# Block-sparse attention with experts: the blocks' own keys first, v by halves of heads, another first batch, and constant products in TensorE's planned waits

## The chip, the cores and the metric

One core of one Trainium2 chip. The metric is the device time of one launch in microseconds (us). TensorE (PE) multiplies matrices and transposes, VectorE (DVE), ScalarE (ACT) and GpSimd (POOL) work on rows, SyncE (SP) issues DMAs; POOL issues DMAs too, on a queue of its own. Each engine works through its own instructions in the order in which the program was written; semaphores hold it where it needs another engine's result or a DMA's.

## The reference

Four batches, eight heads, 768 tokens, 64 channels per head. A token attends to the tokens less than 16 away and to one summary of each of the 24 blocks of 32 tokens (the maximum of k in the block, the mean of v). Each batch then goes to one of eight experts, chosen from its mean.

```python
k_sum = k.reshape(B, H, nb, block, D).max(axis=3)      # block 32, nb 24
v_sum = v.reshape(B, H, nb, block, D).mean(axis=3)
mask_l = np.abs(pos[:, None] - pos[None, :]) < window  # window 16
scores_s = scale * np.einsum('bhsd,bhnd->bhsn', q, k_sum) + np.log(block)
a = softmax(concat([where(mask_l, scale * q @ k^T, -1e9), scores_s]))
x = a @ concat([v, v_sum])                   # then heads side by side: (B, 768, 512)
logits = x.mean(axis=1) @ w_gate             # e = argmax, p = softmax(logits)[e]
out = p * (relu(x @ w1[e]) @ w2[e])          # w1 512x1024, w2 1024x512
```

## The kernel before

Tokens are taken in 12 tiles of 64 queries (j). A tile's keys are a window of 96: its own 64 and 16 on either side. With the 24 block summaries behind them they make 120 rows, so that one product gives all scores of a tile, and one product with v (`av`) the sums and, in a 65th column of ones, the denominators.

A batch passes through these steps, for four pairs of heads:

- **T**: `tk` (line 407) transposes k on TensorE, 16 products into the one PSUM buffer `kps`; `ek` (424 or 426) copies it as overlapping windows to `kT`; `tq` (432) and `eq` (440) do the same for q; `km` (446, DVE) takes each block's maximum of k, `kb` (456, ACT) copies it into each window.
- **Q**, for each half of the tiles (first or second): `qk` (464), 12 products into the one buffer `sc`; `ex` (475, ACT) the exponential; `mk` (479, DVE) the mask.
- **A**, for each half: `av` (497), 12 products into the one buffer `ops`; `nm` (510, 511, DVE) divides by the denominators.
- **X**: `tx` (521) transposes the result back and `xc` (529, ACT) copies it to `xT_b`, with sums for the mean.

For v, `load_v` (213, 216, 225) fetches each head into `v_f`, `cast_v` (299, DVE) makes bf16 of two heads at a time in `vblk`, `halo_v` (304, 305, on SP's queue) copies the 16 border rows of each tile from its neighbours, `vs` (359) sums the blocks on TensorE with the 0/1 matrix `bind`, `ev` (369, DVE) copies the sums out, and `bc` (375, on SP's queue) writes them behind each window. In the first batch 80 rows of each tile come from memory, the 16 before it among them.

The gate of a batch: `lgf` (634) four small products, `mxf` (644 to 649, DVE) the copy and the maximum, `ldf` (654, POOL) reads the index, and POOL issues the chosen expert's loads: w1 (665, in two halves for the first batch) and w2 (671). The experts' step then has 16 groups of hidden products (726, here **h**, four products of 512 or of 256 columns each into one of three buffers `hps`), ReLU on ACT (741), 48 output products (760, **o**, eight to a group), the scaling (770) and the store (773).

`Sched` (lines 22 to 132) sets the order. Each step is an operation with an engine, an estimated time and its predecessors; the planner simulates the engines and writes, at each point, the operation that is ready with the longest remaining tail, so that the expert products of one batch lie among the attention steps of the next. PSUM buffers are booked in the planner (`sch.slot`) and taken from rotating pools in the program. POOL issues the loads of the first batch, then k, q and all of v of the second; two small copies (317, 319) hold the issues of the first batch's k and q until v's heads 2 and 6 have landed. Behind each gate's weights follow the loads of the batch after the next.

## Time and profile before

Three runs took 201.25, 202.06 (the median) and 208.47 us. The profiled execution took 201.35 us by the same clock; from its first to its last instruction its span is 199.8 us.

| | VectorE's copy of the gate's logits | first hidden product after it |
|---|---|---|
| first batch | 44.01 us | 59.18 us |
| second | 77.71 | 95.02 |
| third | 122.07 | 135.42 |
| fourth | 160.22 | 172.93 |

Of the span TensorE is busy 160.0 us (80%), VectorE 100.7, ScalarE 95.7, GpSimd 42.4. The chain of waits that ends last has 55% TensorE and 25% DMA. Times are counted from the span's start. In a list of instructions a row has the start, the duration, the engine, the line, the operation with its output and inputs, a count where several are drawn together, and in brackets how long the engine had been idle and what ended that. In the chain a row has start, duration and what held things up there. A releaser is inferred from semaphores; matmul ends are modelled.

### The profile page before, as it was taken

Reading aid. Unit: us, or ns where it says so; the run is one execution under the profiler, and the core shown is the slowest. Engines: PE = TensorE matmul, PEld = TensorE weight load, DVE = VectorE, ACT = ScalarE, POOL = GpSimd, SP = SyncE. Lnnn points to the kernel's source line nnn. Section 1 sums busy time; section 2 is a strip of 40 time slices with the busy share of each in tenths; the row PEclk is TensorE's granted clock in tenths of the full one; section 3 lists DMA queues with packets and bytes.
Section 4 is the critical chain, followed back from the end, with each engine's and each line's share of the span. In section 5 each row is a group of like instructions: output and inputs, shape, how many; then the busy total and the mean of one; then the engine's idle time right before and its main releaser. Section 6 shows DMA issues by size and latency. Waiting matters only on the chain.

```text
span 199.8 us, 4547 instructions
## 1 busy us (share of the span) xinstructions
PE 160.0 (80%) x1902; PEld 93.0 (47%) x1924; DVE 100.7 (50%) x209; ACT 95.7 (48%) x182; POOL 42.4 (21%) x67
## 2 busy tenths in 40 slices
PE   0342877765989799999999899958999995399992
PEld 0231666544365475434556454334556542156440
DVE  5472488599386789311898781563797210000000
ACT  2203267442057676513778736223888642056431
POOL 6126934007420520911025001100000030000000
PEclk9999999999999999999999999996999999579999
DMA  5999999915999999899999957799200039980142
GB/s 86 210 179 156 178 227 214 166 32 80 178 179 225 198 175 151 138 191 257 267 239 191 184 78 208 147 218 242 39 3 0 3 111 229 260 137 0 56 153 111
DMA packets 28689, 30.45 MB, mean 152 GB/s; under 512 B 9756, under 2 KB 22812, under 8 KB 28572
## 3 DMA queue, kind: packets, MB, share of 16 engines
q0 software_dynamic: 14800, 19.40, 59.6%
q1 hardware_dynamic: 13868, 10.75, 21.3%
q8 instruction: 15, 0.25, 0.5%
q14 instruction: 6, 0.05, 0.1%
HBM read 36.06 MB, written 6.29 MB: 212 GB/s over the span
## 4 chain that ended last, share of the span: by engine, by line
PE 55%; DMA 25%; DVE 6%; SPq 4%; issue 3%; ACT 3%; POOL 2%; POOLq 1%; ACTq 0%
PE hps L726 23%; PE hps L760 15%; DMA w_sb<-in_moe_w_dram 11%; DMA v_f<-in_v_dram 7%; DMA q_nat<-in_q_dram 4%; PE ops L359 4%; PE sc L464 4%; SPq L216 3%; PE ops L497 3%; DMA vblk<-vblk 2%; PE kps L407 2%; PE tps L521 2%; PE tps L432 2%; DVE kT L426 1%; DVE xs L511 1%
## 5 line engine op out<-in xcount | busy, mean ns | idle before, releaser
L726 PE MATMUL hps<-xT_b,w_sb 128*128 128x256 bf16 (+1 forms) x239 | 50.3, 343 | 9.3 <-DMA w_sb<-in_moe_w_dram 7.9
L760 PE MATMUL hps<-w_sb,hT_sb 128*128 128x512 bf16 x187 | 43.4, 380 | 0.3
L741 ACT ACTIVATE hT_sb<-hps 128x512 bf16<-128x512 f32 x64 | 29.8, 490 | 23.4 <-PE hps L726 22.5
L726 PEld LDWEIGHTS <-w_sb 128*128 128x128 bf16 x256 | 23.3, 102 | 24.1 <-DMA w_sb<-in_moe_w_dram 7.9
L475 ACT ACTIVATE aT<-sc 128x768 bf16<-128x768 f32 x32 | 25.9, 809 | 15.7 <-PE sc L464 15.6
L770 ACT ACTIVATE o_sb<-hps,gcol 128x512 f32<-128x512 f32 x24 | 16.5, 687 | 28.2 <-PE hps L760 16.4
L760 PEld LDWEIGHTS <-hT_sb 128*128 128x128 bf16 x192 | 18.0, 98 | 20.5 <-issue 0.9
L213 POOL DMA_DIRECT2D v_f<-in_v_dram x24 | 18.0, 761 | 36.4 <-DMA w_sb<-in_moe_w_dram 26.0
L359 PE MATMUL ops<-vblk,bind 80*32 80x512 bf16 (+1 forms) x60 | 16.3, 445 | 6.0 <-DVE vblk L299 6.0
L479 DVE TENSOR_TENSOR aT<-aT,mask 120x768 bf16<-120x768 bf16 x32 | 17.6, 552 | 4.6 <-ACT aT L475 4.4
L426 DVE COPY kT<-kps 128x1152 bf16<-128x1152 bf16 x12 | 16.2, 1349 | 6.3 <-PE kps L407 6.3
L665 POOL DMA_DIRECT2D w_sb<-in_moe_w_dram x5 | 3.8, 753 | 72.3 <-PE hps L760 51.4
L299 DVE CAST vblk<-v_f 80x1536 bf16<-80x1536 f32 x16 | 14.9, 951 | 7.7 <-DMA v_f<-in_v_dram 7.7
L511 DVE TENSOR_TENSOR xs<-ops,rv 128x384 bf16<-128x384 f32 x32 | 17.8, 558 | 1.1
L407 PE MATMUL kps<-identb,k_nat 96*64 96x96 bf16 x256 | 11.3, 249 | 8.5 <-DMA k_nat<-in_k_dram 7.2
L497 PE MATMUL ops<-vblk,aT 120*64 120x65 bf16 x384 | 13.7, 211 | 4.9 <-DVE xs L511 2.0
L529 ACT ACTIVATE xT_b<-tps 128x768 bf16<-128x768 bf16 x16 | 12.9, 809 | 8.9 <-PE tps L521 8.8
L497 PEld LDWEIGHTS <-aT 120*64 120x64 bf16 x384 | 10.0, 122 | 12.9 <-issue 5.0
L464 PE MATMUL sc<-qT,kT 64*128 64x64 bf16 x384 | 13.1, 210 | 2.9 <-ACT kT L456 1.2
L446 DVE TENSOR_REDUCE kmx<-kT 128x24 bf16<-128x768 bf16 x16 | 15.2, 948 | 0.1
L407 PEld LDWEIGHTS <-k_nat 96*64 96x64 bf16 x256 | 9.2, 139 | 10.6 <-DMA k_nat<-in_k_dram 7.2
L464 PEld LDWEIGHTS <-kT 64*128 64x128 bf16 x384 | 9.2, 105 | 10.0 <-issue 6.4
(55 smaller groups left out, 113.8 us busy)
## 6 DMA issues: line engine op xcount, KB each, us to landing
w_sb<-in_moe_w_dram POOLq DMA_DIRECT2D x7, 1024.0 KB, 15.8
out_dram<-o_sb SPq DMA_DIRECT2D x24, 256.0 KB, 5.1
v_f<-in_v_dram POOLq DMA_DIRECT2D x24, 192.0 KB, 11.2
k_nat<-in_k_dram POOLq DMA_DIRECT2D x6, 384.0 KB, 10.3
q_nat<-in_q_dram POOLq DMA_DIRECT2D x6, 384.0 KB, 11.3
v_f<-in_v_dram SPq DMA_DIRECT2D x7, 240.0 KB, 7.2
vblk<-vblk SPq DMA_DIRECT2D x6, 178.8 KB, 6.2
w_sb<-in_moe_w_dram POOLq DMA_DIRECT2D x2, 512.0 KB, 9.4
```

The costliest lines, as they stand in the source:

```text
L213: nc.gpsimd.dma_start(v_f[16:80, :, h, :], v[b, h].rearrange("(j p) d -> p j d", p=QB))
L359: nc.tensor.matmul(ps[0:32, 0 : n * D], lhsT=bind[:, j, :], rhs=vblks[b % 2][0:80, j, hs, 0:D], start=(j == 0), stop=(j == NJ - 1),)
L407: nc.tensor.transpose(kps[hh * D : (hh + 1) * D, g, 2 : 2 + SP], qk_nat[b][1][:, 2 * pr + hh, g, :], identb[0:SP, 0:SP],)
L426: nc.vector.tensor_copy(kdst, win)
L464: nc.tensor.matmul(sc[:, hh, jj * QB : (jj + 1) * QB], lhsT=sb["kT"][pr][rs, j, :], rhs=sb["qT"][pr][rs, j, :], start=True, stop=True, til ...
L475: nc.scalar.activation(aT, sb["sc"][:, :, 0 : NH * QB], ACT.Exp, scale=SCALE)
L479: nc.vector.tensor_tensor(out=aT[0:NR], in0=aT[0:NR], in1=mask[:, hf * NH : (hf + 1) * NH, :] .rearrange("p j c -> p (j c)") .unsqueeze(1) ...
L497: nc.tensor.matmul(ops[(j % 2) * QB : (j % 2 + 1) * QB, hh, jj // 2, :], lhsT=aT[0:NR, hh, jj * QB : (jj + 1) * QB], rhs=vb[0:NR, j, 2 * p ...
L511: nc.vector.tensor_tensor(out=sb["xs"][pr][:, hf * NS : (hf + 1) * NS, :, :].rearrange("p s h d -> p h s d"), in0=ops[:, :, :, 0:D], in1=r ...
L726: nc.tensor.matmul(sb["hps"][:, 0 : c1 - c0], lhsT=sb["w1"][:, dt, ft * 128 : (ft + 1) * 128], rhs=sb["xT"][:, dt, c0:c1], start=(dt == 0) ...
L741: nc.scalar.activation(sb["hT"][:, ft, c0:c1], ps["t"][:, 0 : c1 - c0], ACT.Relu)
L760: nc.tensor.matmul(ps["t"], lhsT=sb["hT"][:, ft, st * 128 : (st + 1) * 128], rhs=sb["w2"][:, ft, :], start=(ft == 0), stop=(ft == NFT - 1),)
```

## The change

Seven things are changed together.

- The window now begins with the tile's own 64 keys; the border rows stand at 64 to 95. The block sums (`vs`) read the 64 own rows and need the casts alone, no border copy. `ek` becomes two copies (80 and 16 keys of each tile); the masks are built anew.
- `vblk` and the sums are laid out by halves of heads: a border copy moves contiguous 16-row pieces, two for each half; the broadcast is split in two.
- The first batch loads 64 rows per tile, as the others did. Heads 0 and 1 and w_gate go on SP's queue, the other six heads on POOL's, between the pairs of k and q. The small holding copies are gone.
- The first batch's casts of heads 2, 3 and of 6, 7 go to ACT. Its block sums stay in a tile `vs0` of their own at rows 96 to 119, and each half's `av` gets six further products with it (line 573 of the changed kernel) in place of the broadcast.
- The second halves of the first batch use the pool of `hps` for scores (two tiles, two exponentials) and for `av`. A written order replaces the general one in that batch, and the second batch's casts come after all its normalisations.
- `fill` writes products of a constant 128x128 tile (`idle_in`, line 958) where the planner sees TensorE wait. Each such place takes one tile of the `hps` pool, which the planner doesn't book.
- The planner lets an operation follow another of its own engine with no semaphore time, allows an engine a delay (0.9 or 0.6 us) for a more urgent operation, and gives later attention steps and v a priority of 8.

```diff
...
+    FILL_TO = 45.0
+    DELAY = {"PE": 0.9, "DVE": 0.6, "ACT": 0.6}
...
+        busy = t0["PE"]
 
         def push(op):
             r = max(
-                [d["end"] + self.SEM for d in op["deps"]] + [d["issued"] for d in op["after"]],
+                [
+                    d["issued"] if d["eng"] == op["eng"] and not d["dma"] else d["end"] + self.SEM
+                    for d in op["deps"]
+                ]
...
-                    elif (
-                        start + op["dur"] <= pick[0] + 0.1
-                        or (start < pick[0] and tail[pick[1]["n"]] - tail[op["n"]] < self.URGENT)
+                    elif start < pick[0] and (
+                        start + op["dur"] <= pick[0] + self.DELAY.get(eng, 0.1)
+                        or tail[pick[1]["n"]] - tail[op["n"]] < self.URGENT
                     ):
...
+            if eng == "PE":
+                idle = t - busy
+                busy = t + op["dur"]
+                if t < self.FILL_TO:
+                    self.fill(int((idle - 0.4) / (0.1 if t < 8.0 else 0.08)))
+                else:
+                    self.fill(int((idle - 1.2) / 0.08))
...
-    v_f = const_pool.tile([80, NJ, H, D], FP32, name="v_f")
+    v_f = const_pool.tile([QB, NJ, H, D], FP32, name="v_f")
...
+    idle_in = const_pool.tile([128, 128], BF16, name="idle_in")
+    vs0 = const_pool.tile([128, 2, H // 2, D + 1], BF16, name="vs0")
...
     def load_v(b, h):
-        if b > 0:
-            nc.gpsimd.dma_start(v_f[16:80, :, h, :], v[b, h].rearrange("(j p) d -> p j d", p=QB))
-            return
...
+        eng = nc.sync if b == 0 and h < 2 else nc.gpsimd
+        eng.dma_start(v_f[:, :, h, :], v[b, h].rearrange("(j p) d -> p j d", p=QB))
...
+        keep(bind, [[QB, NJ], [-BLK, 32]], 0, 1)
+        keep(bind, [[-QB, NJ], [BLK, 32]], BLK - 1, -1)
...
     def cast_v(b, c, eng):
-        hs = slice(2 * c, 2 * c + 2)
-        dst = vblks[b % 2][0:80, :, hs, 0:D]
+        hs = slice(2 * (c % 2), 2 * (c % 2) + 2)
+        dst = vblks[b % 2][0:QB, c // 2, :, hs, 0:D]
+        src = v_f[:, :, 2 * c : 2 * c + 2, :]
         if eng is nc.scalar:
-            nc.scalar.activation(dst, v_f[:, :, hs, :], ACT.Copy)
+            nc.scalar.activation(dst, src, ACT.Copy)
         else:
-            eng.tensor_copy(dst, v_f[:, :, hs, :])
...
-    def halo_v(b, hs):
+            eng.tensor_copy(dst, src)
+
+    def halo_v(b, g):
+
         vb = vblks[b % 2]
-        if b > 0:
-            nc.sync.dma_start(vb[0:16, 1:NJ, hs, :], vb[64:80, 0 : NJ - 1, hs, :])
-        nc.sync.dma_start(vb[80:96, 0 : NJ - 1, hs, :], vb[16:32, 1:NJ, hs, :])
-
-    v_loads = []
-    for h in range(H):
-        v_loads.append(add("SP", 0.5, [], lambda h=h: load_v(0, h), dma=1.08, after=v_loads[-1:]))
-
...
+        nc.sync.dma_start(vb[QB : QB + 16, g, 0 : NJ - 1, :, :], vb[0:16, g, 1:NJ, :, :])
+        nc.sync.dma_start(vb[QB + 16 : KW, g, 1:NJ, :, :], vb[QB - 16 : QB, g, 0 : NJ - 1, :, :])
+
+    v_loads = [add("SP", 0.5, [], lambda: load_v(0, 0), dma=1.2)]
+    v_loads.append(add("SP", 0.5, [], lambda: load_v(0, 1), dma=1.2, after=v_loads[-1:]))
+
+    def load_wg():
+        nc.sync.dma_start(wg_sb, moe_w_gate.rearrange("(g p) e -> p g e", p=128))
+
+    wg_load = add("SP", 0.5, [], load_wg, dma=0.2, after=v_loads[-1:])
...
+    def pool_v(h):
+        v_loads.append(add("POOL", 0.75, [], lambda: load_v(0, h), dma=0.95, after=[last]))
+        return v_loads[-1]
...
-    tk = add("POOL", 0.2, [v_loads[2], bind_setup], lambda: nc.gpsimd.tensor_copy(tok[:, 0:1], v_f[:, NJ - 1, 2, 0:1]))
-    qk_loads[0, 1] = add("POOL", 1.3, [tk], lambda: load_qk(0, 2, 4), dma=2.3)
-    tk = add("POOL", 0.2, [v_loads[6]], lambda: nc.gpsimd.tensor_copy(tok[:, 1:2], v_f[:, NJ - 1, 6, 0:1]), after=[qk_loads[0, 1]])
-    qk_loads[0, 2] = add("POOL", 1.3, [tk], lambda: load_qk(0, 4, 6), dma=2.3)
-    qk_loads[0, 3] = add("POOL", 1.3, [tk], lambda: load_qk(0, 6, 8), dma=2.3, after=[qk_loads[0, 2]])
-    order_pool = [qk_loads[0, 3]]
...
+    last = pool_v(2)
+    last = pool_v(3)
+    last = keep_setup = add("POOL", 0.9, [], setup_keep, after=[last])
+    last = qk_loads[0, 1] = pool_qk(1)
+    last = bind_setup = add("POOL", 1.2, [], setup_bind, after=[last])
+    last = qk_loads[0, 2] = pool_qk(2)
+    last = pool_v(4)
+    last = pool_v(5)
+    last = pool_v(6)
+    last = pool_v(7)
+    last = qk_loads[0, 3] = pool_qk(3)
...
-            on_act = False
+            on_act = b == 0 and c % 2 == 1
...
+                    after=norms[0] if b == 1 else [],
...
-            def vs(b=b, hs=hs, n=n, st=st):
+            def vs(b=b, g0=g0, g1=g1, n=n, st=st):
                 ps = ops_pool.tile([128, 512], FP32, name="ops")
+                p0 = KW if b == 0 else 0
...
                     nc.tensor.matmul(
-                        ps[0:32, 0 : n * D],
+                        ps[p0 : p0 + 32, 0 : n * D],
                         lhsT=bind[:, j, :],
-                        rhs=vblks[b % 2][0:80, j, hs, 0:D],
+                        rhs=vblks[b % 2][0:QB, g0:g1, j, :, 0:D].rearrange("p g h c -> p (g h) c")
+                        if g1 - g0 == 1
+                        else vblks[b % 2][0:QB, :, j, :, 0:D],
                         start=(j == 0),
...
-            def ev(b=b, n=n, hs=hs, st=st):
+            def ev(b=b, g0=g0, g1=g1, n=n, st=st):
+                dst, src = (
+                    (vs0[KW:NR], st["ps"][KW:NR]) if b == 0 else (vsbs[b % 2], st["ps"][0:NB])
+                )
...
-            win = bass.AP(
-                tensor=full.tensor,
-                offset=full.offset,
-                ap=[list(full.ap[0]), [QB // G, NJ], [1, KW // G], [SP + 4, G]],
...
+            for a0, n, c0 in ((2, 10, 0), (0, 2, 80)):
+                win = bass.AP(
+                    tensor=full.tensor,
+                    offset=full.offset + a0,
+                    ap=[list(full.ap[0]), [QB // G, NJ], [1, n], [SP + 4, G]],
+                )
+                kdst = kT[:, :, c0 : c0 + n * G].rearrange("p j (a g) -> p j a g", g=G)
...
         def av(pr, hf):
             aT = sb["aT"][pr, hf]
-            ops = sb["ops", pr, hf] = ops_pool.tile([128, 512], FP32, name="ops")[
-                :, 0 : 2 * NS * (D + 1)
-            ].rearrange("p (h s c) -> p h s c", h=2, c=D + 1)
+            if second(pr, hf):
+                ops = mps_pool.tile([128, 512], FP32, name="hps")
+            else:
+                ops = ops_pool.tile([128, 512], FP32, name="ops")
...
+            rows = KW if b == 0 else NR
...
                     nc.tensor.matmul(
                         ops[(j % 2) * QB : (j % 2 + 1) * QB, hh, jj // 2, :],
-                        lhsT=aT[0:NR, hh, jj * QB : (jj + 1) * QB],
-                        rhs=vb[0:NR, j, 2 * pr + hh, :],
-                        start=True,
-                        stop=True,
+                        lhsT=aT[0:rows, hh, jj * QB : (jj + 1) * QB],
+                        rhs=vb[0:rows, h // HW, j, h % HW, :],
+                        start=(b > 0 or (hh == 0 and jj < 2)),
+                        stop=(b > 0),
+                    )
+            if b > 0:
+                return
+            for hh in range(2):
+                h = 2 * pr + hh
+                for s in range(NS):
+                    nc.tensor.matmul(
+                        ops[:, hh, s, :],
+                        lhsT=aT[KW:NR, hh, 2 * s * QB : 2 * (s + 1) * QB],
+                        rhs=vs0[KW:NR, h // HW, h % HW, :],
+                        start=False,
+                        stop=(hh == 1 and s == NS - 1),
+                        tile_position=(KW, 0),
                     )
...
-        sch.prio = 40.0 if b == 0 else 0.0
+        sch.prio = 40.0 if b == 0 else 8.0
...
-        sch.prio = 40.0 if b == 0 else 0.0
...
+            sch.prio = 8.0
             casts, bcs = v_ops(nxt, vl)
+            sch.prio = 0.0
...
+    def fill(n):
+
+        if n < 1:
+            return
+        idle = mps_pool.tile([128, 512], FP32, name="hps")
+        for _ in range(n):
+            nc.tensor.matmul(idle[:, 0:128], lhsT=idle_in, rhs=idle_in, start=True, stop=True)
...
```

**GpSimd, the first batch's loads.** Rows name a line, the operation and its output and input; `tok` are the small holding copies. Before:

```order
L206 DMA q_nat<-in_q_dram 96x2x512
...
L246 AFFINE_SELECT bind<-bind 80x384 x3
L317 CAST tok<-v_f 80x1
L206 DMA k_nat<-in_k_dram 96x2x512
...
L319 CAST tok<-v_f 80x1
L206 DMA k_nat<-in_k_dram 96x2x512
...
L213 DMA v_f<-in_v_dram 64x12x64 x8
```

Now:

```order
L229 DMA v_f<-in_v_dram 64x12x64 x2
L249 AFFINE_SELECT mask_116<-mask_116 96x64 x2
L249 AFFINE_SELECT mask_118<-mask_118 96x64
L222 DMA k_nat<-in_k_dram 96x2x512
L222 DMA q_nat<-in_q_dram 96x2x512
L249 AFFINE_SELECT bind<-bind 64x384 x2
L222 DMA k_nat<-in_k_dram 96x2x512
L222 DMA q_nat<-in_q_dram 96x2x512
L229 DMA v_f<-in_v_dram 64x12x64 x4
L222 DMA k_nat<-in_k_dram 96x2x512
```

No issue waits for a landing any more, and six heads of v stand among those of k and q.

**VectorE, the end of the first batch**, from the last cast for that batch's own v (299 before, 309 now) to the gate's copy. Now:

```order
L309 CAST vblk_103<-v_f 64x12x2x64
L537 TENSOR_TENSOR aT<-aT,mask 120x768 x2
L492 TENSOR_REDUCE kmx<-kT_109 128x24
...
L412 CAST vs_112<-ops 24x4x64
...
L486 COPY qT<-tps 128x768
...
L309 CAST vblk_104<-v_f 64x12x2x64 x3
L760 COPY lg<-ops 1x8
```

Before, the row with three casts in front of `lg` was one cast, a normalisation and two casts (`L299 CAST vblk_104`). From the cast that opens this piece on, there are now eight masks, two key maxima, one query copy, one copy of sums, eight normalisations and four casts.

**TensorE around the gate of the third batch**, one row for each group of equal products (weight loads left out). Before:

```order
L634 MATMUL ops<-wg_sb,pooled 1x8 x4
L760 MATMUL hps<-w_sb,hT_sb 128x512
...
L407 MATMUL kps<-identb,k_nat 64x96
...
L688 MATMUL ops<-grec,ones_row 128x1
...
L359 MATMUL ops<-vblk_104,bind 32x512
...
L464 MATMUL sc<-qT,kT_107 128x64
...
L726 MATMUL hps<-xT_b,w_sb 128x512
```

Now:

```order
L750 MATMUL ops<-wg_sb,pooled 1x8 x4
L478 MATMUL tps<-identb,q_nat 64x12x8
...
L452 MATMUL kps<-identb,k_nat 64x96
...
L872 MATMUL hps<-w_sb,hT_sb 128x512
...
L397 MATMUL ops<-vblk_104,bind 32x512
...
L516 MATMUL sc<-qT,kT_108 128x64
...
L842 MATMUL hps<-xT_b,w_sb 128x512
```

Between gate and next h there were three o groups, two `tk`, two `tq`, one `qk` and the block sums; now there are four o groups, three `tk`, three `tq`, four `qk` and the sums. Counted the same way, the second gate has behind it three o groups, three `tk`, three `tq`, four `qk` and the sums (before: two pairs of h groups, six o groups, `tk`, `tq`, sums), and the first gate two `tk`, three `tq`, two `qk`, the sums and 29 constant products. Ahead of the second gate, from that batch's first h, stand now all eight pairs of h groups, six `qk`, two `tk`, one `tq`, eight `av`, four `tx`, three o groups. Ahead of the first gate there are 124 constant products, 74 of them in front of the first block sums.

## Rows read from the trace of the kernel before

**Rows 1.** The chain of waits, first batch: start, duration, what held there.

```profile
13.01 4.94 DMA vblk<-vblk
...
32.24 8.30 DMA q_nat<-in_q_dram
```

**Rows 2.** GpSimd's instructions of the front; the bracket is idle time and releaser.

```profile
18.66 0.63 POOL L206 DMA_DIRECT2D q_nat<-in_q_dram  x1
19.28 1.29 POOL L206 DMA_DIRECT2D k_nat<-in_k_dram  x1
...
21.22 2.99 POOL L213 DMA_DIRECT2D v_f<-in_v_dram  x4
...
46.15 1.50 POOL L665 DMA_DIRECT2D w_sb<-in_moe_w_dram  x2 [13.23 <-DVE grec L685]
```

**Rows 3.** The page's DMA issues: count, KB each, median us to landing.

```profile
v_f<-in_v_dram POOLq DMA_DIRECT2D x24, 192.0 KB, 11.2
...
v_f<-in_v_dram SPq DMA_DIRECT2D x7, 240.0 KB, 7.2
```

**Rows 4.** VectorE's instructions, first batch.

```profile
19.37 0.96 DVE L299 CAST vblk<-v_f 80x1536 bf16<-80x1536 f32 x1 [3.53 <-DMA v_f<-in_v_dram]
...
25.09 0.95 DVE L446 TENSOR_REDUCE kmx<-kT 128x24 bf16<-128x768 bf16 x1
...
29.16 0.55 DVE L479 TENSOR_TENSOR aT<-aT,mask 120x768 bf16<-120x768 bf16 x1
29.62 0.55 DVE L440 COPY qT<-tps 128x768 bf16<-128x768 bf16 x1
```

**Rows 5.** Windows: us, busy PE, PEld, DVE, ACT, POOL, granted clock, DMA, GB/s.

```profile
23.00:44.00 21.00, 15.49 (x317) 12.57 (x318) 15.87 (x32) 12.41 (x20) 5.55 (x8) 1.00 0.99 170
...
95.00:114.00 19.00, 18.27 (x323) 11.05 (x328) 17.05 (x30) 15.51 (x31) 3.60 (x5) 1.00 1.14 222
```

**Rows 6.** VectorE's instructions at the first three gates.

```profile
44.01 0.15 DVE L644 COPY lg<-ops 1x8 f32<-1x8 f32 x1
...
77.71 0.15 DVE L644 COPY lg<-ops 1x8 f32<-1x8 f32 x1
...
115.69 2.68 DVE L299 CAST vblk<-v_f 80x1536 bf16<-80x1536 f32 x3
...
122.07 0.15 DVE L644 COPY lg<-ops 1x8 f32<-1x8 f32 x1 [3.00 <-PE ops L634]
```

**Rows 7.** DMA issues around the first and second gates' w1 loads.

```profile
w_sb<-in_moe_w_dram POOLq DMA_DIRECT2D x1, 512.0 KB, 8.5
...
w_sb<-in_moe_w_dram POOLq DMA_DIRECT2D x1, 1024.0 KB, 13.1
```

**Rows 8.** The chain of waits, from the first gate's block sums to the end.

```profile
49.67 5.23 PE ops L359 x12
...
85.97 2.73 PE ops L359 x12
...
95.02 0.32 PE hps L726
...
95.98 0.28 PE sc L464 x12
...
96.81 0.46 PE tps L432 x16
...
104.96 0.44 PE tps L521 x6
...
115.82 1.73 PE hps L760 x8
...
124.18 10.97 DMA w_sb<-in_moe_w_dram
...
135.42 0.81 PE hps L726 x3
...
172.93 0.61 PE hps L726
```

More of the change, by code (lines that the diff above doesn't have):

```diff
@@ L323 @@
+    mask_setup = add("DVE", 0.9, [keep_setup], setup_mask)
+    sch.prio = 0.0
+    later_setup = add("DVE", 1.0, [], setup_later)
+    sch.prio = 40.0
+    order_pool = [last]
     v_ready = {}
@@ L458, in qk @@
         def qk(pr, hf):
-            sc = sb["sc"] = sc_pool.tile([128, 2, 512], FP32, name="sc")
+            if second(pr, hf):
+                sc = [mps_pool.tile([128, 512], FP32, name="hps") for _ in range(2)]
+            else:
+                whole = sc_pool.tile([128, 2, 512], FP32, name="sc")
+                sc = [whole[:, 0, :], whole[:, 1, :]]
+                sb["sc"] = whole
+            sb["sc", pr, hf] = sc
             for jj in range(NH):
@@ L536, in attention, with second @@
         act_k = b == 0
+        cold = 1.0
+        def second(pr, hf):
+            return b == 0 and hf == 1
         def add_T(pr):
@@ L559, in add_QK @@
             ts, qts, deps = t
-            ss, sd = sch.slot("sc", 1)
-            o_qk = add("PE", 0.34, deps + sd, lambda: qk(pr, hf), lat=0.2)
+            if second(pr, hf):
+                slots = [sch.slot("mps", 3), sch.slot("mps", 3)]
+            else:
+                slots = [sch.slot("sc", 1)]
+            sd = [d for _, ds_ in slots for d in ds_ if d is not None]
+            o_qk = add("PE", 0.34 * cold, deps + sd, lambda: qk(pr, hf), lat=0.2)
             ts["readers"].append(o_qk)
@@ L564, in add_QK @@
             as_, ad = sch.slot("aT", 5)
-            o_ex = add("ACT", 0.82, [o_qk] + ad, lambda: ex(pr, hf))
-            ss["first"], ss["readers"] = o_qk, [o_ex]
+            o_ex = add("ACT", 0.98 if second(pr, hf) else 0.82, [o_qk] + ad, lambda: ex(pr, hf))
+            for sl, _ in slots:
+                sl["first"], sl["readers"] = o_qk, [o_ex]
             as_["first"] = o_ex
@@ L606, in do, with first_sequence @@
                 add_X(pr, XS[pr])
+        def first_sequence():
+            do("T", 0)
+            do("Q", 0, 0)
+            do("Q", 0, 1)
+            do("T", 1)
+            do("A", 0, 0)
+            do("Q", 1, 0)
+            do("A", 0, 1)
+            do("Q", 1, 1)
+            do("T", 2)
+            do("A", 1, 0)
+            do("Q", 2, 0)
+            do("A", 1, 1)
+            do("Q", 2, 1)
+            do("T", 3)
+            do("X", 0)
+            do("A", 2, 0)
+            do("Q", 3, 0)
+            do("A", 2, 1)
+            do("Q", 3, 1)
+            do("X", 1)
+            do("A", 3, 0)
+            do("A", 3, 1)
+            do("X", 2)
+            do("X", 3)
         def sequence():
+            if b == 0:
+                first_sequence()
+                return
             do("T", 0)
```

189 lines of the change are left out of this document (101 added, 88 removed).

## The prediction

> **What bounds it now.** I read the chain of waits first, since it says what each stage ends on, then the lists of VectorE and GpSimd for the front, the windows for how densely an engine can work, and the DMA issues.
>
> The kernel is one chain of four stages. A gate's copy on VectorE releases the index and the weight loads; their landing and TensorE's leftover work release the next batch's h; h and the attention among it end in the next gate. At the first gate the chain runs through border copies (4.94 us) and the last q load of the second batch (8.30 us) [rows 1], because a cast for the second batch's v stands in front of the gate's copy. VectorE meanwhile stands 3.53 us for v [rows 4]. The second stage is TensorE's own work; the last two end on weights (10.97 us at the third gate [rows 8]). So a gate that comes earlier pays fully where weights bind, and TensorE's order decides what hides them.
>
> **First gate, 44.0 to 37.2.** Without holding copies POOL's issues up to v's head 5 are three pairs of k and q (0.63 us each issue) and four v loads (2.99 us [rows 2]); with some 3 us of selects, from a start at 1.5 us, the last of them is out at about 11 us. A first-batch v load took 7.2 us to land, one on POOL's queue 11.2 [rows 3]; the queue is not yet deep, so I take 7.2, and the third cast starts at 18 (from 16 to 22). Behind it VectorE has, in order, what it had between 23 and 44 us, plus one cast (0.96) and two masks (1.10), less one key maximum (0.95) and two query copies (1.10) [rows 4]: no difference, 15.87 us [rows 5]. In that window it was 76% busy, waiting for TensorE's single buffers; between 95 and 114 us it reached 90% [rows 5]. The second halves' own buffers remove part of these waits. So 17.7 to 21.0 us; I take 19.2, and the copy stands at 37.2 instead of 44.01 [rows 6]. The bounds are 33.7 and 43.
>
> The block sums for `vs0` lie in TensorE's waits there (15.49 us busy of 21 [rows 5]), and so do 48 more `av` products. A constant product has no row; its nearest, a 128x128 transpose, is 0.44/6 = 0.07 us [rows 8]. The 74 ahead of the first sums (5.4 us) lie in the wait for the first loads. The other 50 cost 3.7 us where no wait is left and nothing where one is; I take nothing. The split `ek` (16 more copies on ACT and VectorE) is hidden in the later stages, where VectorE has slack.
>
> **First weights and h, 59.2 to 48.1.** The loads were issued 2.14 us behind the copy [rows 2, 6]: 39.3. Their first half landed 8.5 us on [rows 7]; with the second batch's loads still moving it could be the third gate's 10.97 [rows 8]. I take 8.5, 47.8, and 0.3 to the first product, as between 135.15 and 135.42 [rows 8]. TensorE's work in between is five transposes (0.46), two `qk` (0.28) and the sums (2.73): 5.6 us [rows 8], at 2.4 GHz done long before.
>
> **Second gate, 77.7 to 73.7.** The stage from h to the next gate took 27.05 us in the third [rows 6, 8]. It held the same eight pairs of h, eight `av`, four `tx` and three o, but two more `qk` (0.56) and two more transposes (0.92): 25.6 us. This is longer than the stage was (18.5), for work that stood behind the gate has moved ahead of it: the new stage gains 11.1 us at its start and returns 7.1.
>
> **Second h, 95.0 to 87.8.** Behind the gate remain three o (5.2), six transposes (2.8), four `qk` (1.1) and the sums: 11.8 us, where it was 17.3. Now the weights bind: 2.1 us to the issue and 10.97 to 13.1 to land [rows 7, 8], middle 12.0. What was TensorE's bound becomes a wait of 2 us.
>
> **Third gate, 122.1 to 114.** By TensorE the stage loses four `qk`, three transposes and one o against 27.05, 4.2 us, and ends at 110.6. But the copy stands behind the last cast of the fourth batch's v, the copies of one `kT` and a key maximum. The last cast started at 115.69 + 2/3 of 2.68 = 117.5, 39.8 us behind the second gate's copy [rows 6], and all these loads are issued behind that gate: 113.5, and 3.3 us of VectorE work (0.96, about 1.4, 0.95) give 116.8. Since the queue is emptier at the second gate than it was, I take the middle, 114.
>
> **Third h, 135.4 to 127.3.** 13.35 us behind the copy, as before [rows 6, 8]; TensorE's work behind the gate (four o, six transposes, four `qk`, sums: 13.5 us from 110.6) is done earlier, so weights still decide.
>
> **Fourth h and end.** From third to fourth h it was 37.5 us [rows 8], less three transposes, three `qk` and one o (3.95): 160.9. Then the tail, 199.8 - 172.93 = 26.9: a span of 187.8. The profiled execution lies 1.55 above its span: 189.3. It is 0.7 below the median of 202.06, so **190**.
>
> **Rivals.**
>
> *TensorE stays at 1.2 GHz behind the first gate.* The block sums there took 5.23 us against 2.73 later [rows 8], the lower of its levels, after a front in which TensorE had stood and waited. Then the 5.6 us are 11.2 and the 29 constant products up to 4.3, h starts at about 51 and the result is 193. For it speaks that TensorE was 74% busy in that window already [rows 5]; against it, the constant products fill its pauses.
>
> *The front gives nothing.* The third cast at 22 us and VectorE at 76%: the copy at 43 to 44, h at 54.9, gates at 80.5 and about 121, h at 134.1 and 167.7: 197.
>
> *VectorE blocks POOL's issues.* A k load's issue on POOL took 1.29 us where the one before it took 0.63, while a cast ran on VectorE from 19.37 [rows 2, 4]. If all front issues did so, the ten up to head 5 would cost some 7 us more and this is the second rival again, 197. Four v issues side by side with VectorE's work took 2.99, 0.75 each, so I expect two to four such meetings, 1.3 to 2.6 us, inside the bounds above. The Trainium skill (SBUF — State Buffer, Who interferes with whom) says that VectorE in its two-port mode, casts and copies among them, fully blocks GpSimd, its descriptor writing included, and that a queue not fed by GpSimd avoids it. It speaks against moving six heads from SP's queue to POOL's; the one long issue agrees.
>
> *The shared pool turns against it: slower.* Constant products take tiles of the three `hps` buffers, which now also hold the first batch's second halves; the planner doesn't book them. In order on TensorE, such a tile waits until ACT or VectorE has read the one three back. A round of two exponentials, mask, `av` and normalisation is some 3 us; at seven places that is 21, less the 4 us which they were meant to fill: 17, the first gate at 54 and everything behind it 17 later, **207**. It decides from about 2.3 us at each place. Against it: TensorE has a quarter of that window free [rows 5], and VectorE, not TensorE, is behind.
>
> **Chances.** The forecast with its bounds 0.56; TensorE's clock 0.16; the front gives nothing, blocked issues included, 0.18; the shared pool 0.10, half of it at 2 us or less a place, within 2%. A measurement of this kernel tells 2% from no change: below 198.0 is faster, above 206.1 slower. The first two cases and five ninths of the third are faster: 0.82; same 0.13; slower 0.05. The range: cast at 16 (-3.5) and third gate at TensorE's bound (-3.4) give 183; upwards the second rival with the third gate at 116.8 gives 200.
>
> **What would show it.** Right: the first copy at 35 to 39, the first h within 0.5 us of its weights, the second gate at 73 to 75 with all h groups ahead of it, a TensorE wait of about 2 us for weights at the second gate, the third copy right behind a cast chain. Wrong: idle time in front of line 958 with VectorE or ACT as releaser (shared pool); block sums of 5 us behind the first gate (clock); POOL issues of 1.3 us in a row (blocked issues); VectorE's third cast later than 22.

## The result, and the profile after

The changed kernel took 193.9 us (median of four, 193.2 to 198.3) beside 204.0 for the kernel before on the same chip: a ratio of 0.961, 95% interval 0.953 to 0.969. The forecast was 190, range 183 to 200, faster. The profiled execution is the longest of the four (198.26 us, span 196.0; the others have spans of 191 to 193), so it is compared with before stage by stage, and a second trace of the same kernel (experiment 1) stands beside it.

VectorE's third cast for the first batch's v, and its copies at the four gates; columns as in [rows 6], to which the copies answer:

```profile
20.70 0.94 DVE L309 CAST vblk<-v_f 64x1536 bf16<-64x1536 f32 x1
...
46.54 0.15 DVE L760 COPY lg<-ops 1x8 f32<-1x8 f32 x1
...
83.80 0.14 DVE L760 COPY lg<-ops 1x8 f32<-1x8 f32 x1
...
121.52 0.14 DVE L760 COPY lg<-ops 1x8 f32<-1x8 f32 x1
...
154.68 0.15 DVE L760 COPY lg<-ops 1x8 f32<-1x8 f32 x1 [2.44 <-PE ops L750]
```

From copy to copy the second to fourth batches take 37.3, 37.7 and 33.2 us where they took 33.7, 44.4 and 38.2; the last stage takes 41.3, where it took 39.6. In this trace the first copy does not come earlier at all: 46.5 instead of 44.0. All that this execution wins is won between the second and the fourth gate. Its span is only 3.8 us shorter than before, and the trace of experiment 1 is also of a longest execution; in which stages the rest of the median's gain lies, no trace of the change shows.

The windows of the stages; columns as in [rows 5]:

```profile
15.00:45.00 30.00, 28.00 (x437) 21.99 (x436) 16.96 (x35) 15.00 (x29) 8.75 (x12) 0.50 0.90 142
...
20.70:46.50 25.80, 23.81 (x361) 18.70 (x360) 16.13 (x33) 12.65 (x24) 6.03 (x9) 0.50 0.78 127
...
55.70:80.30 24.60, 24.46 (x338) 13.98 (x340) 16.52 (x33) 16.99 (x35) 5.39 (x7) 1.00 1.15 181
83.80:99.40 15.60, 14.50 (x159) 7.25 (x159) 10.87 (x24) 5.33 (x11) 6.77 (x9) 0.67 1.01 187
99.40:121.20 21.80, 21.18 (x296) 12.46 (x294) 15.44 (x31) 15.96 (x33) 3.63 (x5) 1.00 1.07 196
```

The first row is the front. TensorE is busy 28.0 of 30 us there, at a granted clock of 0.50; VectorE, which the forecast took for the limit, is busy 17.0. The second row is the part from the third cast to the first gate's copy: TensorE 23.8 of 25.8 us, VectorE 16.1. The lower clock level is not new in the front: sixteen transposes of k take 0.85 us in the kernel before (first list) as in the change (second list), though the granted clock reads 1.00 there [rows 5] and 0.50 here.

```profile
23.03 0.85 PE L407 MATMUL kps<-identb,k_nat 96*64 96x96 bf16 x16
```
```profile
28.38 0.85 PE L452 MATMUL kps<-identb,k_nat 96*64 96x96 bf16 x16
```

The two window rows with a clock of 1.00 and next to no idle time are the stages from h to gate, full as forecast.

VectorE's last cast for the third batch's v, in front of the second gate's copy, and TensorE's logits of that gate:

```profile
81.59 0.95 DVE L309 CAST vblk<-v_f 64x1536 bf16<-64x1536 f32 x1 [2.13 <-DMA v_f<-in_v_dram]
82.47 1.41 DVE L472 COPY kT<-kps 128x960 bf16<-128x960 bf16 x2
```
```profile
79.98 0.35 PE L750 MATMUL ops<-wg_sb,pooled 128*1 128x8 f32 x8
```

The logits are there at 80.3; the copy stands 3.5 us behind them, for a load, a cast and a copy of `kT` that the gate does not need.

TensorE's list around the first and the last gate:

```profile
13.65 2.71 PE L397 MATMUL ops<-vblk,bind 64*32 64x256 bf16 x12 [3.41 <-ACT vblk L307]
...
38.65 0.37 PE L958 MATMUL hps<-idle_in 128*128 128x128 bf16 x2 [0.57 <-ACT aT L529]
...
49.96 2.80 PE L397 MATMUL ops<-vblk,bind 64*32 64x512 bf16 x12
...
168.31 7.88 PE L842 MATMUL hps<-xT_b,w_sb 128*128 128x512 bf16 x31 [3.96 <-DMA w_sb<-in_moe_w_dram]
```

The block sums behind the first gate take 2.80 us, where the kernel before needed 5.23 [rows 8]. The constant products wait 0.57 us at most for a tile of the shared pool.

### The profile page after: what moved, and what is told of

Its sections match the earlier page's. It is cut to its first block, busy times and chain, and to the rows that moved or that the text cites. A ratio compares the mean times of both kernels' runs of the same rounds, so it can differ in the third digit from the quotient of the medians.

```text
span 196.0 us, 5020 instructions
## 1 busy us (share of the span) xinstructions
PE 175.2 (89%) x2135; PEld 107.0 (55%) x2135; DVE 102.4 (52%) x223; ACT 99.0 (51%) x192; POOL 46.5 (24%) x70
## 4 chain that ended last, share of the span: by engine, by line
PE 58%; DMA 25%; DVE 7%; issue 3%; POOL 2%; ACT 2%; POOLq 1%; DVEq 0%; ACTq 0%
PE hps L842 18%; PE hps L872 14%; DMA v_f<-in_v_dram 10%; DMA q_nat<-in_q_dram 9%; PE ops L397 7%; DMA w_sb<-in_moe_w_dram 6%; PE ops L561 3%; PE sc L516 3%; PE tps L478 3%; PE kps L452 3%; PE tps L598 3%; DVE vblk L309 2%; PE hps L958 1%; PE hps L561 1%; PE hps L573 1%
## 5 line engine op out<-in xcount | busy, mean ns | idle before, releaser
L842 PE MATMUL hps<-xT_b,w_sb 128*128 128x512 bf16 (+1 forms) x256 | 49.2, 340 | 4.9 <-DMA w_sb<-in_moe_w_dram 4.9
L853 ACT ACTIVATE hT_sb<-hps 128x512 bf16<-128x512 f32 (+1 forms) x64 | 29.6, 491 | 16.0 <-PE hps L842 15.7
L842 PEld LDWEIGHTS <-w_sb 128*128 128x128 bf16 x256 | 23.8, 101 | 20.7 <-DMA w_sb<-in_moe_w_dram 5.2
L882 ACT ACTIVATE o_sb<-hps,gcol 128x512 f32<-128x512 f32 x24 | 16.5, 686 | 32.0 <-PE hps L872 22.1
L229 POOL DMA_DIRECT2D v_f<-in_v_dram x30 | 22.7, 766 | 32.4 <-DMA w_sb<-in_moe_w_dram 14.9
L872 PEld LDWEIGHTS <-hT_sb 128*128 128x128 bf16 x192 | 18.0, 99 | 20.7 <-issue 1.5
L397 PE MATMUL ops<-vblk,bind 64*32 64x512 bf16 (+1 forms) x60 | 16.4, 441 | 3.4 <-ACT vblk L307 3.4
L472 DVE COPY kT<-kps 128x960 bf16<-128x960 bf16 (+1 forms) x24 | 16.9, 744 | 2.4 <-PE kps L452 2.4
L958 PE MATMUL hps<-idle_in 128*128 128x128 bf16 x163 | 16.1, 274 | 2.3 <-DVE warm L241 1.2
L588 DVE TENSOR_TENSOR xs<-ops,rv 128x384 bf16<-128x384 f32 x28 | 15.6, 557 | 1.0
L309 DVE CAST vblk<-v_f 64x1536 bf16<-64x1536 f32 x14 | 13.3, 960 | 4.3 <-DMA v_f<-in_v_dram 4.3
L561 PEld LDWEIGHTS <-aT 120*64 120x64 bf16 (+1 forms) x384 | 9.8, 121 | 10.2 <-issue 4.2
L958 PEld LDWEIGHTS <-idle_in 128*128 128x128 bf16 x163 | 13.5, 126 | 3.1 <-DVE warm L241 1.2
L397 PEld LDWEIGHTS <-bind 64*32 64x32 bf16 x60 | 6.8, 118 | 10.7 <-issue 6.4
L587 DVE RECIPROCAL rv<-ops 128x6 f32<-128x6 f32 x28 | 5.4, 192 | 13.4 <-PE ops L561 11.2
```

The source lines that it names most:

```text
L229: eng.dma_start(v_f[:, :, h, :], v[b, h].rearrange("(j p) d -> p j d", p=QB))
L309: eng.tensor_copy(dst, src)
L397: nc.tensor.matmul(ps[p0 : p0 + 32, 0 : n * D], lhsT=bind[:, j, :], rhs=vblks[b % 2][0:QB, g0:g1, j, :, 0:D].rearrange("p g h c -> p (g h) c")
L472: nc.vector.tensor_copy(kdst, win)
L561: nc.tensor.matmul(ops[(j % 2) * QB : (j % 2 + 1) * QB, hh, jj // 2, :], lhsT=aT[0:rows, hh, jj * QB : (jj + 1) * QB], rhs=vb[0:rows, h // ...
L842: nc.tensor.matmul(ps["t"][:, 0 : c1 - c0], lhsT=sb["w1"][:, dt, ft * 128 : (ft + 1) * 128], rhs=sb["xT"][:, dt, c0:c1], start=(dt == 0), ...
```

## The experiments

Each ran on one chip beside the kernel before; 1 to 4, 5 to 8, 9 to 11 and 12 went together. "Copies" are the times of the four gates' copies in its trace. A ratio is to the kernel before. A trace is one execution: the change's own two have first copies 1.5 us apart, and experiments 3 and 12, whose programs are the same up to the last gate, 2.2 us (42.2 and 44.4). Where two traces differ by 2 or 3 us in the front, that alone shows nothing.

**1. The change again.** No edit.

> The changed kernel once more, unchanged, for a second trace beside the experiments that follow. In the trace at hand its TensorE was busy almost without a gap from 13.65 us to the first gate's copy at 46.5, its products at the lower of the two clock levels (block sums of 256 columns 2.71 us for twelve). If that is how the change always runs, the copy stands at 46 to 47 again and the time is 198; if the shorter runs (193.2 to 194.6) differ in the front's clock, a trace of one of them has the copy at 41 to 43, the second gate's copy at 80 or less and all later stages as long as in the trace at hand. If they differ in the second gate's stage only, the first copy is at 46 to 47 and the second at 80.

193.0 us (191.2 to 196.7), ratio 0.960 (0.947 to 0.974). The trace is again of the longest execution (span 194.9): copies 45.1, 81.8, 119.7, 153.2. It has the same granted clock of 0.50 from 15 to 45 us. The copy lies between the times that were expected, so this trace does not tell where the executions differ.

**2. No constant products.** In `fill`:

```diff
-        if n < 1:
+        if n < 1 or n > 0:
             return
```

> All 163 constant products left out, everything else and the order of the rest unchanged. Theory A: the front is TensorE's own work at the lower clock level, and the 50 constant products behind the first block sums (6 us in the trace) are work on that path, which buys nothing: the first gate's copy comes some 5 us earlier (41 to 42), the stretch from gate to first hidden product is longer by 2 to 4 us without the products that filled it, the result is 1 to 3 us under the change (191 to 193). Theory B: they are what brings the clock up when it comes up: without them the block sums behind the first gate take 5.2 us instead of 2.8 and the first hidden products 0.5 us each, and the time is 2 to 5 us over the change (196 to 199).

194.0 us (191.8 to 194.6 and one outlier of 760.6), ratio 0.961 (0.945 to 0.978): the same time, between the two theories. Copies 42.8, 83.5, 122.8, 155.4, span 192.9. The first copy is 2.3 us earlier than in experiment 1, A's direction, but no more than two traces of one front differ. Behind that gate the work runs at the lower clock level and the second stage takes 40.8 us instead of 36.7 (B):

```profile
46.50 5.30 PE L397 MATMUL ops<-vblk,bind 64*32 64x512 bf16 x12
```

And the last stage is 37.5 us instead of 41.7: its granted clock is 1.00 throughout, although TensorE stood 3.45 us for the last weights.

```profile
167.84 10.57 PE L842 MATMUL hps<-xT_b,w_sb 128*128 128x512 bf16 x64 [3.45 <-DMA w_sb<-in_moe_w_dram]
```

That the ten products behind the last gate cost this is not shown: experiment 5 has no constant products either and stands as long, and its 64 products start at the lower level:

```profile
172.86 11.88 PE L731 MATMUL hps<-xT_b,w_sb 128*128 128x512 bf16 x64 [3.45 <-DMA w_sb<-in_moe_w_dram]
```

So the products gain 4 us in the second stage; where they lose it again, since the time is the same, these traces do not settle.

**3. The gap ahead of the first sums filled.** In `fill`:

```diff
+        fills.append(n)
+        if len(fills) == 2:
+            n += 60
```

> Sixty more constant products (90 instead of 30) in the wait for v ahead of the first block sums, where TensorE stood from 10.24 to 13.65 us in the trace; nothing else changed. Theory A (the clock falls in that pause and the front then stays TensorE-bound at the lower level): with the pause filled the block sums take 1.3 to 1.5 us instead of 2.71, the front runs at the upper level, the first gate's copy comes at 38 to 41 and the time is 3 to 6 us under the change. Theory B (the pause does not decide the clock): block sums stay at 2.7, the copy stays at 46, the time is within 1 us of the change.

192.5 us (191.0 to 193.7), ratio 0.963 (0.952 to 0.974): no measurable gain on the change; the copy lies between the two theories. The trace (span 189.4, copies 42.2, 80.2, 116.6, 150.0) shows the mechanism of A and why it brings little:

```profile
13.43 1.51 PE L397 MATMUL ops<-vblk,bind 64*32 64x256 bf16 x12
...
21.87 1.71 PE L397 MATMUL ops<-vblk,bind 64*32 64x256 bf16 x12
23.51 0.85 PE L452 MATMUL kps<-identb,k_nat 96*64 96x96 bf16 x16
```

With the gap filled, the first sums run at the upper level (1.51 us against 2.71), but around 23 us the products fall to the lower one (sixteen transposes 0.85 us, before and later 0.53) with TensorE busy; the granted clock of 25 to 40 us is 0.50. The copy is 2.8 to 4.3 us earlier than in the two traces of the change; in experiment 12, with the same front, 0.7 to 2.2.

**4. Casts behind the gate.** In `v_ops`, `mx` being the operation with the copy:

```diff
-                    after=norms[0] if b == 1 else [],
+                    after=norms[0] if b == 1 else [state[b - 1]["mx"]] if b > 1 else [],
```

> The casts of the third and fourth batches' v are put behind the preceding gate's copy (an order constraint of the planner; the orders of TensorE and VectorE around those gates change with it). Theory A: the second gate's copy at 83.8 us waits for the last cast and its load (VectorE stood 2.13 us for v, and one kT copy follows), while TensorE had the logits at 80.3; without the cast in front the copy stands 3 to 3.5 us earlier there, TensorE does not stand at the gate and does not drop to the lower clock level behind it, and the time is 4 to 7 us under the change. Rival: the weights of that gate then queue behind the same loads, which end no earlier; the h products of the second batch start when they did (99.4), and the time is within 1 us.

202.8 us, ratio 0.999 (0.986 to 1.011): the whole gain is gone. Copies 43.4, 78.3, 120.9, 160.7. The second stage is 34.9 us, 1.8 to 2.3 shorter where A said 3 to 3.5, and the third and fourth are 42.6 and 39.8, 4.7 and 6.3 longer than in experiment 1, which neither theory foresaw. The planner puts less behind such a gate (at the second, two `tk` and two `qk` instead of three and four), and TensorE stands for the weights there, where in the change it did not:

```profile
91.97 1.89 PE L842 MATMUL hps<-xT_b,w_sb 128*128 128x512 bf16 x4 [2.78 <-DMA w_sb<-in_moe_w_dram]
```

and what was not done there comes later, inside the stages that are full: from the second batch's h to the logits' copy TensorE is busy 27.8 us (91.97 to 120.87), in experiment 1 21.2 (97.88 to 119.72). Some of this is the clock, granted at 0.91 over that stretch and at 1.00 in experiment 1's. A gate 3.5 us earlier is worth nothing if the work that hides its weights does not come with it.

**5. The planner's rules alone**, in the kernel before:

```diff
+    DELAY = {"PE": 0.9, "DVE": 0.6, "ACT": 0.6}
...
-                        start + op["dur"] <= pick[0] + 0.1
+                        start + op["dur"] <= pick[0] + self.DELAY.get(eng, 0.1)
...
-        sch.prio = 40.0 if b == 0 else 0.0
+        sch.prio = 40.0 if b == 0 else 8.0
```

> The kernel before with the planner's rules of the change alone (same-engine predecessors without semaphore time, the delays of 0.9 and 0.6 us, priority 8 for later attention and v); layout of v, loads, first batch and masks as before, no constant products. Its order of TensorE around the second, third and fourth gates is the change's, group for group. Theory P (the time is won in the later batches, by what stands ahead of each gate and behind it): the first copy stays at 43 to 45, the second stage takes 37 to 39 us from copy to copy instead of 44.4, the third 33 to 35 instead of 38.2, and the time is 192 to 196, most of the change's gain. Theory F (the order needs the block sums that wait for no border copy, and the front): block sums or av wait for border copies, the stages stay at 42 and 37, the time is 198 to 202.

199.5 us (196.5 to 201.6), ratio 0.994 (0.984 to 1.003). Copies 44.8, 85.5, 126.6, 160.4, span 198.9. The third and fourth stages (the second and third in the expectation's count) fall to 41.1 and 33.8 us; the second grows by 7 to 40.8, since all h groups now stand ahead of its gate. The fourth is as short as P said, the third is not, and both are paid for in the second: the time is F's.

**6. The planner undone**, all else as in the change: the reverse of the edit above.

> The change with the planner's old rules and priorities; the new layout, loads, first batch and constant products stay. The order of later batches goes back to h groups and o groups behind the second gate. Theory P: the later stages take as long as before (44 and 38 us from copy to copy) and the time is 198 to 202. Theory F: the layout and the front carry the gain, and the time is 193 to 196.

200.3 us (197.4 to 207.0), ratio 0.994 (0.986 to 1.002). Copies 41.3, 73.9, 118.1, 155.4, span 197.6: stages of 32.6, 44.2 and 37.3, as before, and a last one of 42.2. Here the stages and the time are P's, in experiment 5 the time was F's, so neither theory holds for both. Taken at their middle, neither half alone gains 1%, and together they gain 3.9%. Without the rules the planner also writes other numbers of constant products.

**7. Further products left out.** In `av`, the loops over `hh` and `s` run over their last value only: 40 of the 48 products are left out, and with them most of the first batch's block sums.

> In the first batch 40 of the 48 further products with the block sums are left out (part of the computation; its output lacks most of the block summaries there). Theory A (the front is TensorE's own work at the lower clock level): 0.078 us each, some 3 us, come off that path, the first copy stands 2.5 to 3.5 us earlier than in the change's second trace (45.1) and the time falls by 2 to 3 us. Rival (they lie in TensorE's waits for VectorE and ScalarE): the copy moves by less than 1 us and the time not at all.

190.0 us (187.7 to 193.2). Copies 41.5, 78.3, 114.2, 148.2, span 187.7: the first copy 3.6 us before that of experiment 1, the second and third stages 36.9 and 35.9 us. This is A's size, but part of it is the clock: the first sums run at the upper level here (1.50 us against 2.71), the granted value from 15 to 45 us was 0.66 and in experiment 1 0.50, and 1.4 of the 3.6 us are won from the first sums to the second, where only five of the 40 stood. That the products lie on the front's path agrees with the trace; how much they cost is not shown apart from the clock.

**8. v back on SP's queue.** In `load_v`:

```diff
-        eng = nc.sync if b == 0 and h < 2 else nc.gpsimd
+        eng = nc.sync if b == 0 else nc.gpsimd
```

> The first batch's six heads of v back on SP's queue, nothing else moved but what the planner makes of it. Theory A (POOL's issues are not what the front waits for: in the change's trace the third cast follows VectorE's own work without a wait, and the issues on POOL took 0.64 to 0.90 us each): the first block sums start within 1 us of where they did, the first copy moves by less than 1.5 us, the time by less than 1.5. Rival (VectorE blocks POOL's issues and v's loads queue behind k and q there): v's heads 2 and 3 land 2 us earlier or more, the first sums start at 11 instead of 13.2 us and the time falls by 2 us or more.

204.3 us (198.6 to 206.8), against 201.2 for the kernel before on that chip: neither theory. The chain of waits and ScalarE's list:

```profile
7.80 0.95 SPq L229
8.79 22.68 DMA v_f<-in_v_dram
```
```profile
31.56 1.50 ACT L307 ACTIVATE vblk<-v_f 64x1536 bf16<-64x1536 f32 x1 [15.87 <-DMA v_f<-in_v_dram]
```

The last head of v, issued at 8.8 us on SP's queue, lands at 31.5, beside all of k and q and the second batch's loads on POOL's; on POOL's queue, in its place between k and q, the last cast started at 20.5 in experiment 1. The first copy falls back to 55.3. With the holding copies gone, v's place in POOL's queue is worth 10 us of the front.

**9. Sums wait for the border copies again.** The 0/1 matrix gets rows 64 to 95 of zeros, and later batches' sums read them:

```diff
-                        else vblks[b % 2][0:QB, :, j, :, 0:D],
+                        else vblks[b % 2][0:KW, :, j, :, 0:D],
```

> The change, but the block sums of the second to fourth batches read the 32 border rows too (against zeros of the 0/1 matrix, so that the sums are the same) and so wait for the border copies again; the planner knows it. Theory L (what the planner's order wins in the later batches needs sums that wait for no border copy, since the planner alone gave under 1%): the sums behind the gates and the av of the next batch come later, the second and third stages from copy to copy take 39 to 41 us instead of 36.7 and 37.9, the time is 196 to 199. Rival (border copies land in 6 us and the sums stand far enough behind the casts; what the planner lacked alone was TensorE's clock behind the first gate, 5.3 us for the sums there instead of 2.8): the stages keep their length within 1 us, the time stays at 192 to 194.

195.7 us (188.3 to 201.5 in ten runs), ratio 0.963 (0.942 to 0.984). Copies 43.9, 84.7, 121.9, 154.5; TensorE stood 1.8 us for a border copy in the middle of the sums, and behind it ran at the lower level:

```profile
51.19 4.87 PE L398 MATMUL ops<-vblk,bind 96*32 96x512 bf16 x11 [1.81 <-DMA vblk<-vblk]
```

The second stage is 40.8 us in this trace, as L said, the third 37.2, as the rival said. The interval is too wide to tell how much of the gain hangs on it; not all of it does.

**10. The broadcast in the first batch too**, in place of the 48 products (`av` over 120 rows, `bc` for each half).

> The change, but the first batch's block sums go behind each window by a broadcast on SP's queue, as in the other batches, and the 48 further products are gone; the output is complete. Theory A (those products are on the front's path at the lower clock level: 3.6 us of the first copy when 40 of them were left out): if the broadcast lands before av needs it (about 6 us behind the copy of the sums; the first av stands 7 us behind it in the change's trace, that of the third pair 7), the first copy comes 2 to 4 us earlier and the time falls by 2 to 3. Rival (the broadcast lands late, behind the loads of the second batch): av waits 2 us or more for it in each half and the time is the change's or more.

196.1 us (193.6 to 198.1), ratio 0.981 (0.968 to 0.994). The first copy is at 47.8:

```profile
23.18 0.55 PE L558 MATMUL hps<-vblk,aT 120*64 120x65 bf16 x12 [5.45 <-DMA vblk<-vsb]
...
39.08 0.55 PE L558 MATMUL hps<-vblk,aT 120*64 120x65 bf16 x12 [5.27 <-issue]
```

The broadcast, issued at 13.7, is late by 5.4 us: the rival, though that the second batch's loads hold it up is not shown. A second stop of 5.3 us has no cause that the profile shows, so of the two stops only the first is the broadcast's.

**11. Constant products at the ends only**: as 3, and the seven places between first sums and first gate left out.

> The change with 90 instead of 30 constant products ahead of the first block sums, and without the 50 in the seven places between them and the first gate; those behind the first gate and the last ten stay. Theory A (inside the front they are work on a path that TensorE sets; behind the gate they are what makes the sums take 2.8 us instead of 5.3): the first copy comes 2 to 4 us earlier than with all of them and the gap filled (42.2), at 38.5 to 40, the second stage still takes 37 to 38 us, the time is 189 to 191. Rival (those inside also carry the clock over the gate): the copy comes at 40 to 41, the sums behind the gate take 4 us or more, the time is 193 or more.

192.4 us (189.0 to 194.7). Copies 43.1, 79.7, 115.7, 148.2, span 187.4; sums behind the gate 2.80 us, so those behind the gate are enough (against the rival). The copy does not come earlier than in 3. TensorE stands 2.27 us in the middle of six equal products:

```profile
32.03 0.23 PE L573 MATMUL hps<-vs,aT 24*128 24x65 bf16 x1
34.53 0.45 PE L573 MATMUL hps<-vs,aT 24*128 24x65 bf16 x5 [2.27 <-issue]
```

Without that stop it might have been at 40.8. A is neither shown nor excluded.

**12. Both gaps filled**: as 3, and 60 instead of 10 behind the last gate.

> The change with 90 instead of 30 constant products ahead of the first block sums, as in the run that filled that gap, and 60 instead of 10 behind the last gate, so that TensorE does not stand for the last weights (2.96 us in that run, behind which the granted clock was 0.77 over the next 7.4 us and the 64 hidden products took 12.26 us). Theory A (what TensorE did before the weights came decides the clock of the last h): no wait of over 0.5 us, granted clock 1.00 there, 64 products in 10.5 to 11, the last stage 37.5 to 38 us instead of 39.4, and the time 1.5 to 2 us below the run with the one gap filled (190.5 to 191). Rival (the clock there falls or not whatever stands ahead: without any constant product it read 1.00 behind a wait of 3.45 us): the granted clock stays at 0.7 to 0.8, the time within 0.7 us of that run (192 to 193).

191.0 us (188.4 to 195.1), ratio 0.950 (0.936 to 0.964), the lowest of all that compute the whole result; its interval overlaps the change's. TensorE's list:

```profile
160.25 3.52 PE L965 MATMUL hps<-idle_in 128*128 128x128 bf16 x60
163.76 10.57 PE L842 MATMUL hps<-xT_b,w_sb 128*128 128x512 bf16 x64
```

The wait is gone, the granted clock is 1.00, 64 products take 10.57 us instead of 12.26, and the last stage takes 37.6 us instead of 39.4: A's numbers. Experiment 2 had the clock of 1.00 without any product, and experiment 5, without any, did not; so filling was enough in this trace, and leaving it out goes either way.

## Why the prediction was right, and where not

- **Direction and size.** Faster, by 3.9% where 6% was forecast; within the range. The mechanism was in part wrong: what the front lost was partly made up by the third gate, where I had taken too much, and that is luck.
- **"First gate, 44.0 to 37.2"**: wrong, by 9.3 us in the profiled execution, 7.9 in experiment 1, 5 to 7 in the edited kernels of experiments 2, 3 and 12. The loads came as forecast (the third cast started at 18.2 to 20.7, without a wait, in the traces of the change and of experiments 2 and 3). What failed is the term behind it: I divided 15.87 us of VectorE work by VectorE's share of 76 to 90%. VectorE's work was right (16.1 us); its share was not. From cast to copy it took 25.8 us (20.70 to 46.54), and TensorE was busy 23.8 of them, at the lower clock level. The rows were there: 15.49 us of TensorE work in 21 [rows 5], at that level too, to which the change adds products. I took nothing for the 48 and the 50; TensorE was busy 4.1 and 6.5 us with them. Leaving out 40 of the 48 brought the copy 3.6 us forward, all constant products together 2.3, both in single traces. Without the constant products it is still 23.3 us from cast to copy, 4 over the forecast, and TensorE busy 82% (experiment 2).
- **"First weights and h"**: 9.2 us from copy to h (55.69), forecast 10.9; the halves of w1 landed in 7.4 us, not 8.5.
- **"Second gate"**: the stage from h was 24.6 us to the logits (55.69 to 80.3), forecast 25.6. That the copy then stands behind v's casts I wrote for the third gate and not for this one: 3.5 us.
- **"Second h"**: forecast 14.1 us behind the copy on weights; 15.6, on TensorE's own work, which ran at a granted clock of 0.67 after the wait at the gate (block sums 5.30 us). Size right, cause wrong.
- **"Third gate"**: I took 114, the middle between TensorE's bound (22.8 us from h) and the loads' (29.0); it was TensorE's: 22.1. Over by 4 us, which cancels almost half of the first gate's error.
- **"Third h", "fourth h" and end**: 13.7, 33.1 and 27.7 us, forecast 13.3, 33.55 and 26.9.
- **The rivals.** *The front gives nothing* held, by its times, in the profiled execution: gates at 80.5 and 121 and h at 134.1 and 167.7, where 83.8, 121.5, 135.2 and 168.3 were measured, and 197 where that execution took 198.3. Its reason, a late cast and VectorE, was wrong, and the median is 3 us below it. *TensorE stays at 1.2 GHz* held for the front and not behind the gate, its place in the forecast, thanks to the constant products there (experiment 2). *The shared pool*: waits of 0.6 us at most. *VectorE blocks POOL's issues*: in the profiled execution the front's issues of k and q took 0.64 to 0.90 us, and taking v off POOL's queue made the front 10 us later, not earlier (experiment 8). By the rule of the Trainium skill (SBUF — State Buffer, Who interferes with whom) a queue that GpSimd does not feed avoids such blocking; in the change there was at most 0.3 us an issue to avoid.
- **What stays open.** The planner's rules and the rest gain under 1% each and 3.9% together. By the traces, the rules shorten the third and fourth stages with either kernel and lengthen the second by 7 us in the kernel before and by 4 in the change. The smaller price in the second stage goes with the clock behind the first gate: it takes 40.8 us in experiments 2, 5 and 9, whose sums there run at the lower level, and 36.7 to 38.0 in the profiled execution and in experiments 1, 3, 11 and 12, whose sums take 2.80 us; between them lie experiment 10 with sums of 4.40 us and 38.1, and experiment 8 with 2.80 and 39.1, whose first h runs at the lower level. This does not explain the joint gain, for experiment 2 pays the whole price and has the same time: its span is 6.0 us below that of experiment 5, with 2.0 us of it ahead of the first gate and 1.8, 1.2 and 1.0 in the third, fourth and last stage. In the third stage of experiment 5 VectorE's casts wait for v, the normalisations stand behind them, TensorE waits for those, and then falls to the lower level (eight products 3.60 us, elsewhere in that trace 1.90):

```profile
113.81 0.96 DVE L304 CAST vblk<-v_f 80x1536 bf16<-80x1536 f32 x1 [3.17 <-DMA v_f<-in_v_dram]
```
```profile
115.51 0.38 PE L502 MATMUL ops<-vblk,aT 120*64 120x65 bf16 x12 [2.17 <-DVE xs L516]
...
118.47 0.54 PE L502 MATMUL ops<-vblk,aT 120*64 120x65 bf16 x12 [1.30 <-DVE xs L516]
...
120.38 3.60 PE L765 MATMUL hps<-w_sb,hT_sb 128*128 128x512 bf16 x8
```

Why the change escapes most of this was not tried, and no run separated the new layout from the new first batch.

## What to carry to other kernels

Before you divide an engine's work by its busy share, look at which engine is next in that window: if the change adds work to it, that one is the limit. Moving work ahead of a gate and behind it is one decision: a gate that comes early without the work that hides its loads returns what it won and more (experiment 4). And test the parts of a joint change in both directions, alone and undone: here both said "nothing", and the whole was worth 4%.

## What the runs showed of the hardware

- The granted clock can stand at 1.00 while products run at the lower of the two levels: experiment 2's sums took 5.30 us in a window of granted clock 1.00, the kernel before's 5.23 us likewise, and the front's sixteen transposes took 0.85 us at 1.00 (before) and at 0.50 (the change). In these traces the durations of equal products tell the level, the column does not.
- In the front of experiment 3 the clock fell while TensorE was working (busy 6.4 of the 8.5 us before, no pause over 0.83); at the last gate it fell behind waits of 2.96 and 3.45 us (experiments 3 and 5) and did not behind another of 3.45 (experiment 2).
- The load of the last head of v took 22.7 us on SP's queue beside a filled POOL queue (experiment 8); on POOL's queue it took 10.4 us in the profiled execution and 7.5 in experiment 1.
- TensorE stood 2.3 and 5.3 us in the middle of equal products with no wait that the profile shows (experiments 11 and 10); what it waited for was not tried.
